# Decay rows in other columns, first weight loads issued earlier, other fillers and new priority tables in a fused attention, gate and MLP kernel

## The chip, the cores and the metric

The kernel runs on one core of one Trainium2 chip. A core has TensorE (PE in the rows; PEld is its weight load), VectorE (DVE), ScalarE (ACT), GpSimd (POOL) and SyncE (SP), which work side by side, each in its own order, and wait for each other by semaphores. DMA engines move data; nearly all transfers here are issued from SP's queue. The metric is the device time of one execution in microseconds; lower is better.

## The reference, cut to what matters

```python
# q, k, v: [4, 8, 576, 64]; s: [4, 8, 576]
scores = q @ k.T / 8                                   # per batch and head
cum = np.cumsum(np.maximum(s, 0), -1)
scores = where(causal, -1e9, scores + np.minimum(-(cum[..., :, None] - cum[..., None, :]), 0))
attn = exp(scores - max(scores)); attn /= sum(attn) + 1e-9
x = (attn @ v) as [4, 576, 512]
gate = sigmoid(sum over k < 5 of conv_w[k] * x shifted by 4 - k tokens)
x = (gate * (x @ w_val)) @ w_out
u = x + (x.T @ U @ V).T                                # U: [576, 32], V: [32, 576]
out = u + relu(u @ w_ch1) @ w_ch2                      # 512 -> 2048 -> 512
```

The weights of all steps behind the attention (conv_w, w_val, w_out, U, V, w_ch1, w_ch2) come as 64-bit numbers, which the kernel turns into pairs of 32-bit ones on the chip ("widening" in what follows). Matrix products are made of three products each: high by high, high by low and low by high part.

## The kernel before, in words

Features lie on the 128 partitions and tokens on the columns. `uT`, a tile of 4 x (4 batches x 576) columns, is where each batch's result is built; columns that no batch uses yet serve as scratch.

**Decay.** The decay bias of a score enters the score product as extra rows: each head's Q and K tile have 64 rows of data and four (two for heads 0 and 1) of decay. For heads 2 to 31 these rows are E and F, made once for all 32 heads from `s` by a cumulative sum (`sp`, `cum`, `ones`) and stored to a DRAM tile `ef`, from where each head loads its own. Before the change `sp` and `cum` lie in batch 1's columns of `uT`, E in batch 2's and F in batch 3's.

**Heads.** A loop over phases n = 0 to 32 emits the scores of head n (`score`, five query tiles, S0 to S4: TensorE product `sc`, DVE maximum `P<-sc`, ACT exp) and, for the head before, its transposes (`trans`, T0 to T4: `pt<-ident,P` on TensorE, then a copy into PTA or PTB). Behind each second head come, for the pair of heads, the product with V (`attn_v`, into `av`, the one PSUM accumulator of its kind), the row sums (`norm_rows`: `rs`, `wrs`), and `norm`: DVE multiplies `av` by the rows into X; POOL splits X into `xh` and `xl`; ACT starts the gate with the first tap into the same accumulator, four DVE taps follow (`av<-X,cw,av`), and ACT's tanh (`uT<-av`) ends it and frees the accumulator. Four pairs are a batch. When a batch's heads are done, its dense work (`values`: x @ w_val and the gate; `outputs`: w_out, U and V) runs between the scores of the next.

**Fillers.** `fill` puts matmuls of zeros (`pt<-causal`) ahead of transposes in the first phases: `fill(bank[key], 2)` for each new tile of transposes and two for each of `norm_rows`, for phases up to 2.

**Side work.** `side_work` is a queue of small steps that widen the weights: conv_w (`craw` to `cw`), then eight chunks of w_val and w_out, U and V, then halves of w_ch1 and w_ch2 (`hraw`). Per 128 x 512 chunk: POOL or ACT scale and limit, four DVE passes (lines 493, 494, 497 and 498 of the kernel before; 504, 505, 508 and 509 of the changed one), three more on POOL. `SIDE` says how many steps a head takes: `[7, 6, 2, 9]` for four ranges of heads. The raw chunks lie in a ring of three, and conv_w beside it, in batch 2's columns of `uT`. The first loads are issued in phases 1 to 3.

**Order.** `Via(kind)` gives each kind of instruction an engine and a priority from the tables PLAN, FIRST (phases up to 8) and LAST (phase 32); a scheduler places the instructions by these priorities. Every instruction that it records has the line of `Via`'s call, 250 before and 255 after, so rows are told apart by their tiles. SP issues loads in its own order, and each engine executes in order.

**MLP.** Behind the last head the MLP runs to the end, from about 350 us on; its first part overlaps with the last heads' work.

Of the kernel before, what the change touches and what calls it, by code (L numbers as in the profile page):

```python
# [20 lines left out]


PLAN = {'pace': ['gpsimd', 0],
 'qk_hi': ['gpsimd', 500],
 'qk_lo': ['gpsimd', -2000],
 'put': ['sync', 2000],
 'wd_rest': ['gpsimd', -500],
 'xh': ['gpsimd', 2000],
 'xl': ['gpsimd', 2000],
 'gh': ['scalar', 0],  # L30
 'gl': ['vector', -6000],
 'uh': ['vector', 500],
 'ul': ['gpsimd', -500],
 'u4': ['vector', 100],
 'wd_a': ['scalar', 0],
 'wd_lim': ['gpsimd', 500],
# [6 lines left out]
 't': ['tensor', 100],
 'pt10': ['scalar', 6000],
 'pt20': ['scalar', -6000],
 'pt30': ['scalar', 100],
 'pt40': ['scalar', -500],
 'pt41': ['vector', 100],
 'av': ['tensor', 2000],
 'rs': ['vector', 100],  # L50
 'wrs': ['gpsimd', 6000],
 't_rb': ['tensor', 500],
 'rb': ['scalar', -2000],
 'x': ['vector', 500],
 'tap0': ['scalar', 2000],
 'tap': ['vector', -2000],
 'tanh': ['scalar', 2000],
 'd': ['tensor', -2000],
 'gv': ['vector', 500],
 'ox': ['scalar', 2000],  # L60
 'tm': ['tensor', 0],
 'nh': ['scalar', 0],
 'nl': ['vector', 100],
 'ah': ['vector', 100],
 'al': ['vector', 100],
 'um': ['vector', 500],
 'c1': ['tensor', -2000],
 'c2': ['tensor', -6000],
 'hh': ['scalar', -100],
 'hl': ['vector', 2000],  # L70
 'acc': ['vector', -100],
 'tc': ['vector', -6000],
 'th': ['scalar', 2000],
 'tl': ['vector', 2000],
 'sc': ['gpsimd', -2000],
 'sh': ['scalar', 100],
 'sl': ['gpsimd', 6000],
 'sn': ['scalar', 2000],
 'sa': ['vector', -6000],
 'tu': ['tensor', 6000],  # L80
 'tv': ['tensor', -500],
 'fetch': ['sync', -6000],
 'te': ['vector', 0],
 'tle': ['gpsimd', 2000],
 'the': ['scalar', -500]}
# [14 lines left out]
PACE = 1  # L100
PLACE = [[0, 2, 1, 4, 3], [0, 1, 4, 2, 3], [4, 0, 1, 2, 3], [2, 3, 0, 1, 4]]
PACED = False
SIDE = [7, 6, 2, 9]
WHOLE = [0, 1, 2, 3, 4, 5, 6, 7, 16, 30]
XB = 1
FIRST = {'pt41': ['scalar', -6000],
 'nl': ['vector', 500],
 'xh': ['gpsimd', 0],
 'c2': ['tensor', 0],
# [4 lines left out]
 'av': ['tensor', 6000],  # L114
 'wd_rest': ['gpsimd', -2000],
 'ah': ['scalar', -500],
 'pt10': ['scalar', 100],
 'al': ['vector', -500],
 'xl': ['gpsimd', 500],
 'pt40': ['scalar', -6000],  # L120
# [3 lines left out]
 'gh': ['scalar', 500],  # L124
 'hl': ['vector', 0],
 'wd_hi': ['gpsimd', -500],
 'u4': ['gpsimd', -500],
 'pt20': ['scalar', 2000],
 'pace': ['gpsimd', 500],
 'tm': ['tensor', 2000],  # L130
# [8 lines left out]
 'tc': ['gpsimd', -2000],  # L139
 'sn': ['vector', -6000],  # L140
 'sh': ['vector', -500],
 'tu': ['tensor', -6000],
 'tv': ['tensor', 0],
 'qk_hi': ['gpsimd', 100],
 'th': ['scalar', -2000],
# [2 lines left out]
 'ox': ['vector', 500],  # L148
 'wd': ['vector', 0],
 'tanh': ['scalar', 6000],  # L150
 'exp': ['scalar', 0],
 'hh': ['scalar', -2000],
 'ul': ['gpsimd', 6000],
 'sl': ['vector', 0],
 'acc': ['vector', 2000],
 'te': ['gpsimd', -2000],
 'tap0': ['scalar', -6000],
 'wd_lo': ['gpsimd', 2000],
 'tl': ['vector', 2000],
# [41 lines left out]
DT = {'exp': 0.71,
 'xh': 0.51,
 'xl': 1.47,
 'tap': 2.23,
 'taps': 0.51,
 'tanh': 1.21,
 'gv': 1.47,
 'nl': 3.07,
 'rows': 9.44,
 'prep': 3.98}  # L210
WARM = 13


@with_exitstack
def fused_kernel(ctx, tc, qT, kT, vP, s, wval, wout, convw, U, V, w1, w2, rows01, out):
# [495 lines left out]
    def norm_rows(pr):  # L711
        force("sc")
        sm = sums[pr % 2]
        rs = at1.tile([P, 5, 2], F32, tag="rs", name="rs", bufs=2)
        Via("rs").tensor_scalar_add(rs, sm, 1e-9)
        Via("rs").reciprocal(rs, rs)
        wide_rs = at1.tile([P, 5, P], F32, tag="wrs", name="wrs")
        rnd("wrs", wide_rs.rearrange("p c (e d) -> p c e d", e=2), rs.unsqueeze(3).to_broadcast([P, 5, 2, 64]))
        ready.add(("rows", pr))
        RB = RBs[pr] = wide_rs.rearrange("p c q -> p (c q)")[:, 0:S]  # L720
        for lo, hi, cs in ((0, SA, (0, 1, 2)), (SA, S, (3, 4))):
            ps = psD.tile([P, 512], F32, tag="d", name="pt")
            fill(ps, 2)
# [660 lines left out]
```

## Time and profile before

| | |
|---|---|
| time, median of 3 runs | 738.66 us (737.77 to 739.78) |
| profiled execution's own time | 739.64 us |
| span of the profile | 737.9 us |
| mean granted TensorE clock | 0.981 of full speed |
| busy: PE, DVE, ACT, POOL | 711.0, 566.9, 323.5, 242.4 us |
| DMA | 92.96 MB, mean 126 GB/s |

The span is from the first to the last instruction; the execution's own time has launch and end around it. Busy time counts instructions of an engine, idle time ahead of one is put down to what it waited for, and PEclk is the share of full clock that TensorE was granted.

### The profile page before, as it was taken

To read this page: it belongs to the slowest core of one execution; us is meant where nothing else is said; L and a number is where in the kernel's file an instruction comes from. 1 tells how busy PE (TensorE), PEld (TensorE's weight loads), DVE (VectorE), ACT (ScalarE), POOL (GpSimd) and SP (SyncE) were. 2 spreads that over 40 slices of the span, in tenths; PEclk is the share of its full clock that TensorE was granted. 3 is DMA by queue.
4 is the path that set the end of the run, shared out by engine and by line. 5 is a ranking of instruction groups with operands and counts; after the bars stand their busy time and mean duration, and the time that the engine had idled before them with its cause. 6 is when DMAs were issued, how large, how long until landed. Compare 5 with 4: busy or idle time off the path is not lost.

```text
span 737.9 us, 12465 instructions
## 1 busy us (share of the span) xinstructions
PE 711.0 (96%) x4395; PEld 600.6 (81%) x4395; DVE 566.9 (77%) x1279; ACT 323.5 (44%) x786; POOL 242.4 (33%) x269
## 2 busy tenths in 40 slices
PE   8987899899899999999999999999999999999997
PEld 4765799679888999799878888888888888888886
DVE  6688797878778765783599888898989899686454
ACT  5676476746667667752242222322222223132220
POOL 2567577645453433378060111011020111001000
PEclk8898999979999999999999999999999999999999
DMA  4675555744566553035201222616327062350063
GB/s 129 193 203 152 148 144 141 184 113 111 145 154 155 148 131 92 33 96 190 87 1 57 89 84 74 240 58 229 113 86 257 29 225 91 106 177 1 15 213 143
DMA packets 43130, 92.96 MB, mean 126 GB/s; under 512 B 6440, under 2 KB 7080, under 8 KB 43068
## 3 DMA queue, kind: packets, MB, share of 16 engines
q1 hardware_dynamic: 43068, 92.17, 41.9%
q8 instruction: 35, 0.57, 0.3%
q14 instruction: 27, 0.22, 0.1%
HBM read 66.40 MB, written 9.50 MB: 103 GB/s over the span
## 4 chain that ended last, share of the span: by engine, by line
PE 80%; DVE 9%; DMA 4%; ACT 4%; POOL 2%; issue 1%; SPq 0%; POOLq 0%; ACTq 0%
PE d L250 36%; PE acc L250 26%; PE av L250 6%; PE pt L250 5%; PE sc L250 5%; DMA uT<-in_w 2%; DVE P L250 1%; DVE av L250 1%; POOL uT L250 1%; DVE sn L250 1%; DMA K<-Q 1%; ACT P L250 1%; PE pt L830 1%; DVE uT L250 1%; DVE uT L493 1%
## 5 line engine op out<-in xcount | busy, mean ns | idle before, releaser
L250 DVE TENSOR_TENSOR uT<-acc,uT 128x512 f32<-128x512 f32 (+1 forms) x160 | 96.0, 629 | 29.2 <-PE acc L250 28.4
L250 PE MATMUL acc<-hl,w2h 128*128 128x512 f32 (+1 forms) x320 | 103.8, 370 | 0.0
L250 PE MATMUL acc<-hh,w2l 128*128 128x512 f32 (+1 forms) x320 | 102.8, 371 | 0.0
L250 PE MATMUL acc<-hh,w2h 128*128 128x512 f32 (+1 forms) x320 | 102.1, 371 | 0.0
L250 PE MATMUL sc<-K,Q 68*128 68x288 f32 (+13 forms) x384 | 92.7, 353 | 1.8 <-ACT PTB L250 1.1
L250 PE MATMUL d<-u,w1h 128*128 128x512 f32 (+1 forms) x320 | 84.1, 350 | 0.0
L250 DVE CUSTOM_DVE_ANT_0 P<-sc,causal 64x64 f32<-64x64 f32 (+4 forms) x160 | 65.0, 421 | 23.5 <-PE sc L250 22.9
L250 PE MATMUL pt<-ident,P 128*128 128x128 f32 x400 | 66.6, 287 | 8.4 <-DVE nm L250 3.4
L250 POOL TENSOR_SCALAR scr<-raw 128x512 f32<-128x512 f32 x28 | 20.0, 715 | 157.0 <-DVE w1l L250 80.6
L250 ACT ACTIVATE P<-P,nm 64x64 f32<-64x64 f32 (+4 forms) x115 | 63.8, 557 | 17.0 <-DVE nm L250 16.7
L250 PEld LDWEIGHTS sc<-K,Q 68*128 68x128 f32 (+2 forms) x384 | 63.2, 198 | 8.8 <-DVE nm L250 1.9
L250 PEld LDWEIGHTS acc<-hh,w2h 128*128 128x128 f32 x320 | 59.1, 188 | 11.7 <-ACT Sh L257 0.4
L250 PEld LDWEIGHTS acc<-hh,w2l 128*128 128x128 f32 x320 | 59.1, 188 | 11.2
L250 PEld LDWEIGHTS acc<-hl,w2h 128*128 128x128 f32 x320 | 59.0, 188 | 11.0 <-DVE hl L250 0.2
L250 PEld LDWEIGHTS pt<-ident,P 128*128 128x128 f32 x400 | 48.7, 146 | 18.9 <-ACT P L629 5.2
L250 PEld LDWEIGHTS d<-u,w1h 128*128 128x128 f32 x320 | 56.0, 188 | 9.2 <-DVE hl L250 0.2
L250 ACT ACTIVATE hh<-sn 128x512 fp32r<-128x512 f32 x47 | 28.8, 630 | 67.8 <-DVE sn L250 50.9
L250 DVE SCALAR_TENSOR_TENSOR av<-X,cw,av 128x576 f32<-128x576 f32 x64 | 52.2, 815 | 4.8 <-ACT av L250 4.4
L250 PE MATMUL d<-u,w1l 128*128 128x512 f32 (+1 forms) x160 | 55.8, 349 | 0.0
L250 ACT ACTIVATE sn<-d 128x512 f32<-128x512 f32 x39 | 23.3, 597 | 72.2 <-PE d L250 69.5
L250 POOL TENSOR_TENSOR Sl<-scr,Sh 128x512 fp32r<-128x512 f32 x14 | 18.5, 1327 | 95.6 <-ACT Sh L257 95.6
L250 ACT ACTIVATE hh<-d 128x512 fp32r<-128x512 f32 (+1 forms) x41 | 20.8, 511 | 62.6 <-PE d L250 34.7
(187 smaller groups left out, 1690.8 us busy)
## 6 DMA issues: line engine op xcount, KB each, us to landing
raw<-in_w SPq DMA_DIRECT2D x28, 512.0 KB
Eh<-te SPq DMA_DIRECT2D x48, 256.0 KB
El<-te SPq DMA_DIRECT2D x48, 256.0 KB
V<-in_vP SPq DMA_DIRECT2D x16, 576.0 KB
K<-hi SPq DMA_DIRECT2D x44, 144.0 KB
Q<-hi SPq DMA_DIRECT2D x44, 144.0 KB
out<-uT SPq DMA_DIRECT2D x16, 256.0 KB
qk<-in_qT SPq DMA_DIRECT2D x22, 144.0 KB
```

The lines of the kernel that those rows point to most:

```text
L250: return f(*args, **kw)
L493: lambda: Via("wd").tensor_scalar(tu, au, 3, None, op0=ALU.logical_shift_left),
L830: Via("tm").transpose(ps[:, m * P:(m + 1) * P], uT[:, m, s0:s0 + P], ident)
```

## The change

- `sp` and `cum` go into a tile `early` in a PTB buffer, `ones` into a PTA buffer; E and F go into the columns of batches 0 and 1. The columns of the ring and of `craw` are so free from the start.
- conv_w and the first two chunks of w_val (`SOON = 2`) are issued in the code ahead of the store of `ef`; the scheduler puts a third chunk there too. Side steps are also taken in phase 0.
- `SIDE` becomes `[9, 8, 2, 9]`.
- `FILL = [4, 3, 1]`: four fillers for a tile of transposes, and only in phases up to 1; the three of `norm_rows` never come, since it runs from phase 2 on. Twenty fillers become twelve.
- `ORDER0`, PLAN, FIRST, LAST and the scheduler's delays DT have other numbers; some kinds change engine.

```diff
-PLAN = {... 'wd_a': ['scalar', 0], 'wd_lim': ['gpsimd', 500], 'tap': ['vector', -2000], ...}
+PLAN = {... 'wd_a': ['scalar', 2000], 'wd_lim': ['gpsimd', 6000], 'tap': ['vector', -500], ...}
...
+SOON = 2
-SIDE = [7, 6, 2, 9]
+SIDE = [9, 8, 2, 9]
...
-ORDER0 = 'S0 T0 T1 T4 S1 S2 T3 T2 S3 S4'
+ORDER0 = 'S0 S1 T0 T4 T1 S2 T2 T3 S3 S4'
...
-DT = {'exp': 0.71, 'xh': 0.51, 'tap': 2.23, 'tanh': 1.21, 'gv': 1.47, 'prep': 3.98, ...}
+DT = {'exp': 0.93, 'xh': 0.43, 'tap': 2.2, 'tanh': 0.99, 'gv': 2.35, 'prep': 1.43, ...}
+FILL = [4, 3, 1]
...
-    sp, cum = (part(1, m, parts=NH) for m in range(2))
-    ones = part(1, 2)
+    early_t = at.tile([P, 5 * (S - SA)], F32, tag="PTB", name="early")
+    sp, cum = (early_t[0:NH, m * S:(m + 1) * S] for m in range(2))
+    ones = at.tile([P, 4 * DA], F32, tag="PTA", name="ones")[:, 0:S]
-    E = [part(2, r, parts=NH) for r in range(KP)]
-    F = [part(3, r, parts=NH) for r in range(KP)]
+    E = [part(0, r, parts=NH) for r in range(KP)]
+    F = [part(1, r, parts=NH) for r in range(KP)]
...
+    ring = [uT[:, m, 2 * S:2 * S + 1024] for m in range(3)]
+    craw = uT[:, 3, 2 * S + 1024:2 * S + 1064]
+    nc.sync.dma_start(craw.bitcast(U32), convw.bitcast(U32))
+    for i in range(SOON):
+        nc.sync.dma_start(ring[i].bitcast(U32), wval.bitcast(U32)[i * P:(i + 1) * P, :])
     for i in range(2):
         nc.sync.dma_start(ef[:, i], EF[i])
...
-        if phase[0] <= 2:
+        if phase[0] <= FILL[2]:
...
-            fill(bank[key], 2)
+            fill(bank[key], FILL[0])
...
-        if n == 1:
-            nc.sync.dma_start(craw.bitcast(U32), words(convw))
-        if 1 <= n <= 3:
+        if max(1, SOON) <= n <= 3 and n > SOON:
             load_wide(n - 1)
...
-            if n > 0:
+            if n > 0 or SOON:
                 steps[0] += SIDE[(n > 8) + (n > 12) + (n > 17)] * cost / total
```

Where the order changes, three places are shown, as they stand in the two programs. The first is SP's queue near the start, behind the loads of Q and K of heads 0 and 1; `V` is the value tile of heads 0 and 1, the loads from `in_qT` and `in_kT` are head 2's. Before:

```order
L418 DMA V<-in_vP 128x1152
L473 DMA ef<-uT 32x4x576 x2
L407 DMA Q_196<-in_qT 64x576
L408 DMA K_197<-in_kT 64x576
L413 DMA Q_196<-uT 4x1x576
L413 DMA K_197<-uT 4x1x576
L925 DMA uT<-in_convw 128x40
L521 DMA uT<-in_wval 128x1024 x2
```

After:

```order
L480 DMA uT<-in_convw 128x40
L482 DMA uT<-in_wval 128x1024 x2
L424 DMA V<-in_vP 128x1152
L530 DMA uT<-in_wval 128x1024
L484 DMA ef<-uT 32x4x576 x2
L413 DMA Q_209<-in_qT 64x576
L414 DMA K_210<-in_kT 64x576
L419 DMA Q_209<-uT 4x1x576
L419 DMA K_210<-uT 4x1x576
L530 DMA uT<-in_wval 128x1024
```

conv_w and two chunks now stand ahead of V, a third ahead of the store of `ef`, and a fourth behind head 2's rows.

The second is DVE within the second pair's taps; `X_94` is that pair's product, `av<-X_94,cw,av` its taps, the `ISA P_..` rows are maxima of a head's query tiles and the `ISA nm` rows their results. Before, from behind the second of four taps on:

```order
L250 ISA P_88,nm<-sc,causal 64x64
L250 ISA nm 64x1
L493 TENSOR_SCALAR uT<-uT 128x512
L250 ISA P_92,nm<-sc,causal,nm 128x288
L250 ISA nm 128x1
L250 SCALAR_TENSOR_TENSOR av<-X_94,cw,av 128x576
L494 SCALAR_TENSOR_TENSOR uT<-uT 128x512
L250 ISA P_89,nm<-sc,causal 128x192
L250 ISA nm 128x1
L250 ISA P_90,nm<-sc,causal 128x320
L250 ISA nm 128x1
L250 SCALAR_TENSOR_TENSOR av<-X_94,cw,av 128x576
```

After, from behind the first tap on:

```order
L255 ISA P_88,nm<-sc,causal 64x64
L255 ISA nm 64x1
L255 SCALAR_TENSOR_TENSOR av<-X_94,cw,av 128x576
L255 ISA P_92,nm<-sc,causal,nm 128x288
L255 ISA nm 128x1
L255 SCALAR_TENSOR_TENSOR av<-X_94,cw,av 128x576
L255 ISA P_89,nm<-sc,causal 128x192
L255 ISA nm 128x1
L504 TENSOR_SCALAR uT<-uT 128x512
L255 ISA P_90,nm<-sc,causal 128x320
L255 ISA nm 128x1
L255 SCALAR_TENSOR_TENSOR av<-X_94,cw,av 128x576
```

Two widening passes stood between the taps; now one does, ahead of the last.

The third is TensorE at the start of the products of `values` for batch 0, where `xh_943` (before) and `xh_962` (after) belong to the fourth pair and the others to the first three. Before:

```order
L250 MATMUL d<-xh_405,wvh 128x288
L250 MATMUL d<-xl_406,wvh 128x288
L250 MATMUL d<-xh_405,wvl 128x288
L250 MATMUL d<-xh_577,wvh 128x288
L250 MATMUL d<-xl_578,wvh 128x288
L250 MATMUL d<-xh_577,wvl 128x288
L250 MATMUL d<-xh_746,wvh 128x288
L250 MATMUL d<-xl_747,wvh 128x288
L250 MATMUL d<-xh_746,wvl 128x288
L250 MATMUL d<-xh_943,wvh 128x288
```

After, from behind the first 24 products of the same kind on:

```order
L255 MATMUL d<-xh_761,wvh 128x288
L255 MATMUL d<-xl_762,wvh 128x288
L255 MATMUL d<-xh_761,wvl 128x288
L255 MATMUL d<-xh_413,wvh 128x288
L255 MATMUL d<-xl_414,wvh 128x288
L255 MATMUL d<-xh_413,wvl 128x288
L255 MATMUL d<-xh_588,wvh 128x288
L255 MATMUL pt<-ident,P_88 128x128
L255 MATMUL pt<-ident,P_89 128x128
L255 MATMUL pt<-ident,P_90 128x128
L255 MATMUL d<-xh_962,wvh 128x288 x3
```

The first product with the fourth pair's `xh` was the tenth; now 31 products of the first three pairs stand ahead of it.

## Rows read from the trace of the kernel before

**Rows 1.** Cores view: span and mean granted clock.
```profile
core 0: 737.9 us, clock 0.981
```

**Rows 2.** Windows by stage: us, busy PE, PEld, DVE, ACT, POOL, PEclk, DMA share, GB/s.
```profile
8.60:13.20 4.60, 3.39 (x18) 2.10 (x17) 4.06 (x18) 3.73 (x11) 0.00 (x0) 0.99 0.46 102
13.20:23.40 10.20, 10.20 (x39) 7.67 (x37) 3.39 (x19) 5.86 (x20) 2.28 (x5) 0.50 0.69 204
23.40:38.00 14.60, 14.60 (x110) 10.65 (x108) 12.04 (x36) 9.94 (x29) 9.68 (x12) 1.00 0.53 162
...
67.70:74.60 6.90, 4.67 (x34) 3.37 (x34) 5.22 (x13) 3.37 (x9) 4.54 (x5) 0.51 0.68 179
...
84.00:145.00 61.00, 59.79 (x502) 53.51 (x500) 49.76 (x139) 43.88 (x123) 43.01 (x50) 1.00 0.58 147
145.00:149.70 4.70, 2.72 (x15) 1.65 (x13) 3.90 (x14) 2.39 (x8) 2.39 (x3) 1.00 0.62 134
149.70:160.00 10.30, 9.48 (x42) 6.91 (x41) 6.40 (x18) 4.17 (x13) 3.11 (x5) 0.50 0.25 69
...
350.00:700.00 350.00, 349.18 (x1678) 289.57 (x1677) 289.73 (x514) 97.91 (x172) 50.12 (x50) 1.00 0.31 106
```

**Rows 3.** Waits of PE, 24 to 84 us: in total, times, longest.
```profile
PE av L250 <- ACT uT L250: 3.7, 3, 2.2
PE pt L250 <- ACT P L629: 2.7, 4, 1.3
PE d L250 <- POOL xh L250: 2.5, 1, 2.5
```

**Rows 4.** Timeline, 9 to 24 us: start, duration, instruction, idle time before it.
```profile
19.73 0.53 PE L250 MATMUL sc<-K,Q 68*128 68x64 f32 x2
...
20.44 0.16 DVE L493 TENSOR_SCALAR uT<-uT 128x20 uint32<-128x20 uint32 x1
...
21.29 0.17 DVE L501 TENSOR_TENSOR cw<-uT 128x20 f32<-128x20 f32 x1
21.33 1.06 PE L250 MATMUL pt<-causal 128*128 128x256 bf16 x4
```

**Rows 5.** Tile causal as PE's operand (fillers): ns min/median/max, first and last start.
```profile
L250 PE MATMUL pt<-causal x20: 269/352/421, 10.6 to 28.5; 128*128 128x256 bf16 x20
```

**Rows 6.** Windows of 2 us near the start, columns as in rows 2.
```profile
8.00:10.00 2.00, 1.66 (x6) 0.76 (x4) 1.93 (x3) 0.62 (x1) 0.00 (x0) 1.00 0.05 21
...
18.00:20.00 2.00, 2.00 (x9) 1.47 (x8) 0.99 (x4) 0.76 (x3) 0.41 (x2) 0.50 0.98 338
```

**Rows 7.** Timeline, 49 to 72 us: widening passes, third product, tanh, attn_v.
```profile
51.32 0.68 DVE L494 SCALAR_TENSOR_TENSOR uT<-uT 128x512 uint32<-128x512 uint32 x1
...
59.13 0.74 DVE L250 TENSOR_TENSOR X<-av,wrs 128x576 f32<-128x576 f32 x1
...
62.77 1.39 DVE L494 SCALAR_TENSOR_TENSOR uT<-uT 128x512 uint32<-128x512 uint32 x1
...
67.51 0.68 DVE L498 SCALAR_TENSOR_TENSOR uT<-uT 128x512 f32<-128x512 uint32 x1
...
70.39 0.65 ACT L250 ACTIVATE uT<-av 128x576 f32<-128x576 f32 x1 [0.84 <-DVE av L250]
...
71.09 1.12 PE L250 MATMUL av<-PTA,V 128*64 128x256 f32 x4 [2.23 <-ACT uT L250]
```

**Rows 8.** Timeline, 77 to 84 us: products of batch 0 and the fourth xh.
```profile
79.03 0.29 PE L250 MATMUL d<-xh,wvh 128*128 128x288 f32 x1
...
80.09 0.29 PE L250 MATMUL d<-xh,wvl 128*128 128x288 f32 x1
...
82.14 0.67 POOL L250 TENSOR_SCALAR xh<-X 128x576 fp32r<-128x576 f32 x1
...
82.86 0.54 PE L250 MATMUL d<-xh,wvh 128*128 128x288 f32 x2 [2.49 <-POOL xh L250]
```

**Rows 9.** Timeline, 140 to 150 us: ACT at a w1 half.
```profile
147.17 0.43 ACT L257 ACTIVATE uT<-uT 128x256 f32<-128x256 f32 x1 [2.16 <-DMA uT<-in_w]
```

More of the change, by code (lines that the diff above doesn't have):

```diff
@@ L23 @@
 PLAN = {'pace': ['gpsimd', 0],
- 'qk_hi': ['gpsimd', 500],
- 'qk_lo': ['gpsimd', -2000],
+ 'qk_hi': ['gpsimd', -6000],
+ 'qk_lo': ['gpsimd', -100],
  'put': ['sync', 2000],
@@ L29 @@
  'xl': ['gpsimd', 2000],
[L30 to L36, printed above, removed]
+ 'gh': ['scalar', -500],
+ 'gl': ['vector', 100],
+ 'uh': ['vector', 2000],
+ 'ul': ['gpsimd', 500],
+ 'u4': ['vector', -100],
+ 'wd_a': ['scalar', 2000],
+ 'wd_lim': ['gpsimd', 6000],
  'wd': ['vector', 0],
@@ L42 @@
  'exp': ['scalar', 100],
[L43 to L50, printed above, removed]
+ 't': ['tensor', 6000],
+ 'pt10': ['scalar', 0],
+ 'pt20': ['scalar', 2000],
+ 'pt30': ['scalar', -6000],
+ 'pt40': ['scalar', 0],
+ 'pt41': ['vector', -500],
+ 'av': ['tensor', 100],
+ 'rs': ['vector', 500],
  'wrs': ['gpsimd', 6000],
  't_rb': ['tensor', 500],
- 'rb': ['scalar', -2000],
+ 'rb': ['scalar', 0],
  'x': ['vector', 500],
  'tap0': ['scalar', 2000],
- 'tap': ['vector', -2000],
+ 'tap': ['vector', -500],
  'tanh': ['scalar', 2000],
@@ L59 @@
  'gv': ['vector', 500],
- 'ox': ['scalar', 2000],
+ 'ox': ['scalar', 6000],
  'tm': ['tensor', 0],
- 'nh': ['scalar', 0],
- 'nl': ['vector', 100],
+ 'nh': ['scalar', 2000],
+ 'nl': ['vector', 0],
  'ah': ['vector', 100],
[L65 to L71, printed above, removed]
+ 'al': ['vector', 6000],
+ 'um': ['vector', 0],
+ 'c1': ['tensor', 2000],
+ 'c2': ['tensor', -500],
+ 'hh': ['scalar', -500],
+ 'hl': ['vector', 100],
+ 'acc': ['vector', -500],
  'tc': ['vector', -6000],
- 'th': ['scalar', 2000],
+ 'th': ['scalar', 0],
  'tl': ['vector', 2000],
- 'sc': ['gpsimd', -2000],
+ 'sc': ['gpsimd', -500],
  'sh': ['scalar', 100],
  'sl': ['gpsimd', 6000],
- 'sn': ['scalar', 2000],
- 'sa': ['vector', -6000],
+ 'sn': ['scalar', -100],
+ 'sa': ['vector', 6000],
  'tu': ['tensor', 6000],
  'tv': ['tensor', -500],
[L82 to L85, printed above, removed]
+ 'fetch': ['sync', 100],
+ 'te': ['vector', 6000],
+ 'tle': ['vector', 0],
+ 'the': ['scalar', 0]}
 R0 = 0.31
@@ L116 @@
  'ah': ['scalar', -500],
- 'pt10': ['scalar', 100],
+ 'pt10': ['scalar', 2000],
  'al': ['vector', -500],
@@ L126 @@
  'wd_hi': ['gpsimd', -500],
- 'u4': ['gpsimd', -500],
+ 'u4': ['gpsimd', -100],
  'pt20': ['scalar', 2000],
@@ L141 @@
  'sh': ['vector', -500],
- 'tu': ['tensor', -6000],
+ 'tu': ['tensor', 6000],
  'tv': ['tensor', 0],
@@ L150 @@
  'tanh': ['scalar', 6000],
- 'exp': ['scalar', 0],
+ 'exp': ['scalar', -2000],
  'hh': ['scalar', -2000],
@@ L155 @@
  'acc': ['vector', 2000],
- 'te': ['gpsimd', -2000],
+ 'te': ['vector', -2000],
  'tap0': ['scalar', -6000],
@@ L160 @@
  'sc': ['vector', -500],
- 'tle': ['gpsimd', 6000],
- 't_rb': ['tensor', 6000]}
-ORDER0 = 'S0 T0 T1 T4 S1 S2 T3 T2 S3 S4'
+ 'tle': ['vector', 6000],
+ 't_rb': ['tensor', 6000],
+ 'uh': ['vector', -6000],
+ 's': ['tensor', 500]}
+ORDER0 = 'S0 S1 T0 T4 T1 S2 T2 T3 S3 S4'
 ORDER = 'T0 S0 T1 T3 T2 S1 S2 S3 T4 S4 A0 A1'
@@ L171 @@
  'c2': ['tensor', -6000],
- 'acc': ['vector', -500],
+ 'acc': ['vector', 6000],
  'sh': ['scalar', 0],
  'c1': ['tensor', -500],
- 'sc': ['vector', 500],
+ 'sc': ['vector', -6000],
  'nh': ['scalar', 100],
@@ L180 @@
  'wd_lo': ['vector', -2000],
- 'tc': ['vector', -2000],
- 'wd_lim': ['vector', -6000],
+ 'tc': ['vector', 100],
+ 'wd_lim': ['vector', 0],
  'tl': ['vector', -6000],
- 'hl': ['vector', 100],
+ 'hl': ['vector', 0],
  'the': ['scalar', 500],
  'pt10': ['vector', 6000],
- 'ul': ['gpsimd', 500],
+ 'ul': ['gpsimd', 6000],
  'sl': ['gpsimd', -100],
@@ L192 @@
  'ah': ['scalar', 0],
- 'hh': ['scalar', -100],
+ 'hh': ['scalar', -2000],
  'sn': ['scalar', 100],
- 'wrs': ['vector', 2000],
+ 'wrs': ['gpsimd', 2000],
  'tle': ['gpsimd', 6000],
@@ L198 @@
  'te': ['gpsimd', -6000],
- 'xh': ['scalar', 6000]}
+ 'xh': ['scalar', 6000],
+ 'qk_hi': ['gpsimd', -6000]}
 NPD = 6
-DT = {'exp': 0.71,
- 'xh': 0.51,
+DT = {'exp': 0.93,
+ 'xh': 0.43,
  'xl': 1.47,
[L204 to L207, printed above, removed]
+ 'tap': 2.2,
+ 'taps': 0.58,
+ 'tanh': 0.99,
+ 'gv': 2.35,
  'nl': 3.07,
  'rows': 9.44,
- 'prep': 3.98}
+ 'prep': 1.43}
 WARM = 13
+FILL = [4, 3, 1]
 @with_exitstack
@@ L378, in fused_kernel @@
         nc.scalar.activation(x[64:66, :], x[64:66, :], AF.Relu)
-    EF = [uT[0:NH, :, b * S:(b + 1) * S] for b in (2, 3)]
+    EF = [uT[0:NH, :, b * S:(b + 1) * S] for b in (0, 1)]
     hd = {}
@@ L515, in fused_kernel @@
     scr = [uT[:, 3, 2 * S + i * 512:2 * S + (i + 1) * 512] for i in range(2)]
-    craw = uT[:, 3, 2 * S + 1024:2 * S + 1064]
-    ring = [uT[:, m, 2 * S:2 * S + 1024] for m in range(3)]
     def rows(w, src, c):
@@ L722, in norm_rows @@
             ps = psD.tile([P, 512], F32, tag="d", name="pt")
-            fill(ps, 2)
+            fill(ps, FILL[1])
             for c in cs:
```

2 lines of the change are left out of this document (1 added, 1 removed).

## The prediction

> **What bounds the kernel now.** I read the span and the clock first [rows 1]: 737.9 us at a mean granted clock of 0.981. The profiled execution's own time is 739.64 us, so 1.74 us lie around the span; the median of the runs shown is 738.66 us, 1.0 below this execution. I make the sum against 739.64 and take 1.0 off at the end.
>
> Next comes the table by stage [rows 2]. From 350 to 700 us TensorE (PE) is busy for 349.18 of 350 us, and from 84 to 145 us for 59.79 of 61. There nothing on another engine can be gained or, within limits, lost. Time can only come from TensorE's own work, from its idle time in the first 84 us and around 145 us, and from the three stretches in which PEclk reads 0.50 or 0.51. That is the lower of its two levels, 1.2 instead of 2.4 GHz. What TensorE did there would have taken half as long at the upper level, so the three cost half of its busy time: 10.20/2 = 5.1 us (13.2 to 23.4), 4.67/2 = 2.3 (67.7 to 74.6) and 9.48/2 = 4.7 (149.7 to 160), together 12.1 us. Each follows a stage in which TensorE idled: it was busy for 3.39 of 4.60 us before the first and for 2.72 of 4.70 before the third [rows 2].
>
> Third, whom TensorE waits for between 24 and 84 us [rows 3]: 3.7 us, in three waits, for the tanh on ACT that ends a pair's gate and so frees the one attn_v accumulator; 2.7 us for exps; 2.5 us, in one wait, for the split xh on POOL (GpSimd). These are the waits that the change can reach.
>
> **The change, part by part.**
>
> *Earlier loads.* The E and F rows move out of the columns that the ring of raw weights uses, so conv_w and three w_val chunks (0.52 MB each, 128 x 1024 words of 4 bytes) are issued ahead of the store of ef and of head 2's Q and K. They then lie in a hole: from 8 to 10 us the DMA engines are busy for 0.05 of the time [rows 6]. Three chunks are 1.57 MB; at the 338 GB/s that the same rows show from 18 to 20 us that is 4.7 us of transfer, begun at about 8 us and so done at about 13. Head 2's first score runs at 19.73 us [rows 4]. I cost the loads at nothing. If that cover were gone, head 2 would start up to 4.7 us late.
>
> *conv_w's passes.* The five small DVE passes that widen conv_w take 0.87 us, from 20.44 to the end of the one at 21.29 [rows 4], where TensorE is the bound. They move to the head of the program: two stand ahead of head 0's first maximum, three among its maxima. There the chain scores, maxima, exps has nothing to hide them. Two of five are 0.35 us, all five 0.87. I take **+0.6**. The first also comes to depend on conv_w's load (rival E).
>
> *Filler matmuls.* Twenty of 128 x 256 become twelve. The twenty lie between 10.6 and 28.5 us, with a median of 352 ns [rows 5]; at half clock four in a row took 1.06 us, 0.265 each [rows 4]. In the order before, four stand ahead of head 0's first transposes, ten more up to those of head 1, and six behind; after, eight stand ahead of head 0's first, where TensorE idles, and four more up to head 1's. So six fewer run in the slow stretch, in which TensorE was busy for all of 10.20 us [rows 2]: 6 x 0.265 = 1.6. The bounds are 0, if TensorE then waits for exps instead, and 8 x 0.265 = 2.1. I take **-1.5**. The last six I cost at nothing, since waits lie beside them; without these waits they would add at most 6 x 0.13 at full clock.
>
> *Widening earlier and faster* (SIDE from 7 to 9 steps a head, and from head 0). DVE is in order, so a 128 x 512 pass between two taps puts off the tanh, and with it the next pair's attn_v. In the third pair the product is at 59.13, the tanh at 70.39, and attn_v starts at 71.09 after 2.23 us of idle time [rows 7]. By the order before, two widening passes stand between the first pair's product and its last tap, two in the second pair, four in the third; after: none, one, three. The second pair loses the pass that took 0.68 (at 51.32); of the third I take the one at 67.51, also 0.68, since the 1.39 of 62.77 stays in another place [rows 7]. Both fit into waits: of the 3.7 us for tanh [rows 3] 2.2 are the third pair's and 1.5 remain for the other two. With 0.7 + 0.7, and 0.2 for the first pair, whose wait is the smallest, I take **-1.6**. The bounds are 0 (the pairs' maxima put off the last tap instead) and all of 3.7.
>
> *Order of the dense work of batch 0.* Before, nine products of `values` stand ahead of the first that needs the fourth xh. They start at 79.03 and 80.09 (first and last: 0.133 apart), then TensorE waits for POOL, whose xh starts at 82.14 and lets it go on at 82.86, after 2.49 us [rows 8]. After, 31 products that need only the first three pairs stand ahead: 31 x 0.133 = 4.1 us, where 82.86 - 79.03 = 3.8 are wanted. So the wait is covered: **-2.4**. The bounds are 0, if POOL's xh comes later by as much, and -2.5. What is behind it runs with TensorE nearly full from 84 us on [rows 2], so the gain is kept.
>
> *The rest.* PTA copies going from ACT to DVE, the limits and raw copies on POOL, the tables for the heads after 84 us, and the changed priorities of the MLP I cost at nothing, because TensorE is full there; if that cover failed, single waits of half a microsecond would show. The three slow stretches I leave where they are, since what precedes each stays: the wait for the first exps, the third pair's maxima, and the load at 145 us.
>
> Sum: 0.6 - 1.5 - 1.6 - 2.4 = -4.9; 739.64 - 4.9 = 734.7, and 1.0 less is **733.7 us**.
>
> **The rivals.** Two times within 0.3% (2.2 us) I count as the same: from 736.4 to 740.9 us.
>
> *B. One slow stretch goes as well.* The third follows a wait of ACT: the ACTIVATE at 147.17 sits 2.16 us idle for the load of a w1 half, with exps behind it [rows 9]. In the new order load and ACTIVATE stand among other work; with five ACT instructions more between them the wait would be gone, and with it the idle time before the clock falls. For the first stretch, four more fillers stand in the idle time before it. Against: the load is still issued one step ahead of its first use, and four fillers at full clock fill little of the 1.2 us idle in the 4.60 [rows 2]. It gives 4.7 to 5.1 us more: 733.7 - 5 = 728.7.
>
> *C. The gains are not there.* TensorE's waits for tanh and xh are replaced by waits for exps, because DVE and POOL get 9 steps of widening a head instead of 7 and the maxima queue behind them. For: the exps already cost 2.7 us [rows 3]. Against: TensorE has the work to cover it in `values`. Only the fillers' 1.5 less 0.6 remain: about 738.
>
> *D. The clock stays low beyond 23.4 us: slower.* Between 13.2 and 23.4 us the fillers fill TensorE's gaps, and the clock rose after a stretch in which it was busy for all of 10.20 us [rows 2]. With six fewer it may show gaps there and stay at 1.2 GHz. From 23.4 to 38 us it is busy for all 14.60 us [rows 2], so each further microsecond at half clock costs half a microsecond. To lose 4.9 + 2.2 it must stay low for 14 us more; two more lengths of 10.2 give +10.2 and 743.9, one length 738.8. Against: the scores and transposes alone queue there, and DVE waits for them. The Trainium skill (TensorE: Matmul & The Clock Gate, HAM oscillation) says that waits which leave TensorE idle in a loop send its clock down again, each time it has recovered. What it would make of the time here is D's 743.9, and by it taking out fillers is a step in the wrong direction. The trace agrees in so far as the falls follow stages with idle time, but it shows the fall at 13.2 with the fillers in place.
>
> *E. conv_w comes late.* DVE's second instruction on it stands ahead of head 0's first maximum. If its load lands behind the Q and K rows of both heads, DVE waits and all of the prologue with it. Landing 3 to 4 us late gives 733.7 + 3.5 = about 737. Against: it is issued ahead of the chunks and is small.
>
> **How the numbers follow.** Forecast A 0.45 (730.5 to 736.4 by its terms' bounds), B 0.20, C 0.18, D 0.10, E 0.07. The likeliest gives 733.7. For 8 in 10 the range must take in B and C and the short form of D: 727 to 740.5, which leaves out some 0.07 below (two stretches gone, or one with the full bounds) and 0.12 above. Faster: A and B, 0.65; same: most of C and E, and the short form of D, 0.20; slower: the long D and the worst of C, 0.15.
>
> **What would show it.** Right: the fillers' busy time between 13 and 24 us falls by about 1.5 us; TensorE's wait for the third pair's tanh falls from 2.23 to about 1.5, and the one for the fourth xh from 2.49 to under 0.3; the three slow stretches are still there and begin within 5 us of where they were, less what was gained ahead; behind 160 us nothing differs by more than 1 us. Wrong: a stretch at half clock more or fewer, a DVE wait for conv_w ahead of the first maximum, waits of TensorE for exps that grow by what those for tanh shrink, or idle time of TensorE in the MLP.

## The result, and the profile after

The changed kernel takes 730.57 us (median of 6 runs, 728.65 to 731.72) against 739.12 us of the kernel before (6 runs, 737.77 to 740.09): ratio 0.9883, interval 0.9862 to 0.9904. That is 8.5 us less, where 4.9 were worked out. The direction and the range held; much of the size came from places where the prediction had put nothing. A ratio, here and below, leaves out runs more than 1.5% above the fastest of their program, and it is not the quotient of the two medians.

The cores view of the changed kernel's profile and two of its windows by stage, with the columns and limits of [rows 2]:

```profile
core 0: 729.3 us, clock 0.988
```

```profile
84.00:145.00 61.00, 55.59 (x449) 48.97 (x448) 48.86 (x136) 39.75 (x114) 37.10 (x44) 1.00 0.58 147
...
350.00:700.00 350.00, 349.21 (x1676) 289.71 (x1675) 291.41 (x515) 96.64 (x169) 48.71 (x49) 1.00 0.32 108
```

The span fell by 8.6 us [rows 1]. The MLP from 350 us on is what it was, 349.21 us busy of 350. The stage from 84 to 145 us is less full than before, 55.59 against 59.79 us [rows 2]. There are again three stretches at half clock, 1.7 to 5.1 us earlier than before, and two of them are shorter. Their own windows:

```profile
11.44:14.85 3.41, 3.41 (x14) 2.29 (x13) 2.32 (x12) 3.16 (x13) 1.27 (x2) 0.50 0.93 334
66.05:69.46 3.41, 2.89 (x26) 2.13 (x28) 0.89 (x4) 1.34 (x3) 2.80 (x4) 0.50 0.70 215
144.56:154.80 10.24, 9.80 (x44) 7.30 (x42) 6.51 (x23) 4.16 (x12) 2.91 (x5) 0.50 0.21 59
```

10.2, 6.8 and 10.2 us at the lower level have become 3.4, 3.4 and 10.2. By half of TensorE's busy time they cost 12.1 us before and (3.41 + 2.89 + 9.80)/2 = 8.1 after. The difference is half of what the span lost, and the prediction had left it at zero.

TensorE's waits from 24 to 84 us in the changed kernel, beside [rows 3]:

```profile
PE av L255 <- ACT uT L255: 4.6, 2, 3.9
PE pt L255 <- ACT P L255: 1.3, 2, 1.1
...
PE d L255 <- POOL xl L255: 0.2, 1, 0.2
```

The wait for the fourth xh (2.5 us) is gone; 0.2 us for its low part is left. The waits for exps halved. Those for tanh, from which I expected 1.6 us, grew from 3.7 to 4.6: the longest, the third pair's, grew from 2.2 to 3.9, and the others fell from 1.5 to 0.7 together. The timeline of the third pair shows how, beside [rows 7]:

```profile
53.59 0.75 DVE L255 TENSOR_TENSOR X<-av,wrs 128x576 f32<-128x576 f32 x1
...
57.31 1.35 POOL L255 TENSOR_SCALAR uT<-uT 128x512 f32<-128x512 f32 x2
...
58.69 0.43 DVE L504 TENSOR_SCALAR uT<-uT 128x512 uint32<-128x512 uint32 x1 [1.55 <-POOL uT L255]
...
59.73 1.41 POOL L255 TENSOR_TENSOR xl<-X,xh 128x576 fp32r<-128x576 f32 x1
...
60.34 1.35 DVE L505 SCALAR_TENSOR_TENSOR uT<-uT 128x512 uint32<-128x512 uint32 x1
...
65.87 0.65 ACT L255 ACTIVATE uT<-av 128x576 f32<-128x576 f32 x1 [1.43 <-DVE av L255]
...
66.57 2.19 PE L255 MATMUL av<-PTA,V 128*64 128x256 f32 x20 [3.89 <-ACT uT L255]
```

The product (X) stands 5.5 us earlier than in [rows 7], and the tanh only 4.5. DVE sits idle for 1.55 us at 58.69, in its order, for POOL's scaled chunk of 57.31, and the tap behind it is late; three passes stand between taps, as the order said, and the second of them takes 1.35 us. TensorE's wait for this tanh grew from 2.23 to 3.89 us.

The products of `values` for batch 0, beside [rows 8]:

```profile
76.64 0.67 POOL L255 TENSOR_SCALAR xh<-X 128x576 fp32r<-128x576 f32 x1
...
78.24 0.29 PE L255 MATMUL d<-xh,wvh 128*128 128x288 f32 x1
...
78.62 0.64 PE L255 MATMUL d<-xh,wvh 128*128 128x288 f32 x3
```

The 31st product begins at 78.24, and the first with the fourth pair's xh at 78.62 has no wait, for POOL began that xh at 76.64.

The second place where time came from lies behind the ninth pair's product, at about 180 us. TensorE's waits from 150 to 230 us, before and then after:

```profile
PE pt L250 <- DVE nm L250: 1.2, 2, 0.9
PE sc L250 <- ACT PTB L250: 1.1, 1, 1.1
PE pt L250 <- ACT P L250: 0.7, 2, 0.4
PE pt L830 <- DVE nm L250: 0.5, 1, 0.5
PE av L250 <- ACT uT L250: 0.4, 1, 0.4
PE d L250 <- ACT PTB L250: 0.2, 1, 0.2
```

```profile
PE av L255 <- ACT uT L255: 0.5, 1, 0.5
PE d L255 <- DVE gvl L255: 0.2, 1, 0.2
PE sc L255 <- DMA qk<-in_kT: 0.2, 1, 0.2
PE pt L255 <- DVE nm L255: 0.2, 1, 0.2
```

Together 4.1 us before, of which 0.8 lie ahead of that product, and 1.1 after, all behind it. What moved is seen at one half of the MLP's weights. Before, on ACT and then on TensorE:

```profile
191.39 0.43 ACT L257 ACTIVATE uT<-uT 128x256 f32<-128x256 f32 x1 [3.74 <-DMA uT<-in_w]
191.73 0.47 ACT L250 ACTIVATE PTB<-pt 128x384 f32<-128x384 f32 x1
```

```profile
192.26 0.54 PE L250 MATMUL sc<-K,Q 68*128 68x288 f32 x2 [1.07 <-ACT PTB L250]
```

After, on ACT:

```profile
185.28 0.44 ACT L255 ACTIVATE uT<-uT 128x256 f32<-128x256 f32 x1 [2.75 <-DMA uT<-in_w]
185.62 0.39 ACT L255 ACTIVATE gvh<-d 128x288 fp32r<-128x288 f32 x1
```

In both kernels ACT waits some 3 us for the load of a half. Before, the copy into PTB is the next instruction on ACT, and TensorE waits 1.07 us for it; after, another instruction stands there, and TensorE has no wait. The tables, which I had costed at nothing because TensorE was full, are the likeliest cause; e4 and e7 below bear on it.

### The profile page after: what moved, and what is told of

The parts are those of the page before. It is cut to its first block, busy times and chain, and to the rows that moved or that the text cites. A ratio compares the mean times of both kernels' runs of the same rounds, so it can differ in the third digit from the quotient of the medians.

```text
span 729.3 us, 12465 instructions
## 1 busy us (share of the span) xinstructions
PE 706.5 (97%) x4387; PEld 597.8 (82%) x4387; DVE 563.2 (77%) x1282; ACT 319.6 (44%) x780; POOL 246.3 (34%) x272
## 4 chain that ended last, share of the span: by engine, by line
PE 80%; DVE 8%; DMA 5%; POOL 3%; ACT 2%; issue 1%; SPq 0%; POOLq 0%; ACTq 0%; DVEq 0%
PE d L255 37%; PE acc L255 26%; PE av L255 6%; PE sc L255 5%; PE pt L255 5%; DMA uT<-in_w 2%; DVE P L255 1%; DMA qk<-in_kT 1%; DVE av L255 1%; DVE sn L255 1%; DMA K<-Q 1%; POOL uT L255 1%; DVE uT L504 1%; PE pt L839 1%; POOL Q L255 1%
## 5 line engine op out<-in xcount | busy, mean ns | idle before, releaser
L255 PE MATMUL acc<-hl,w2h 128*128 128x512 f32 (+1 forms) x320 | 106.2, 371 | 0.0
L255 ACT ACTIVATE P<-P,nm 128x576 f32<-128x576 f32 (+4 forms) x160 | 88.9, 557 | 34.3 <-DVE nm L255 33.6
L255 PEld LDWEIGHTS sc<-K,Q 68*128 68x128 f32 (+2 forms) x384 | 61.4, 194 | 11.8 <-DVE nm L255 4.6
L255 PE MATMUL pt<-ident,P 128*128 128x128 f32 x400 | 64.4, 279 | 3.8 <-ACT P L255 1.9
```

Source lines behind the costliest of these rows:

```text
L255: return f(*args, **kw)
```

## The experiments

The runs came in three groups, each on one chip with runs of the kernel before between them; its medians there were 738.49 (31 runs, 730.71 to 742.95), 738.05 (29 runs, 731.37 to 743.78) and 737.16 us (17 runs, 729.86 to 742.59). So single executions of one program lie 12 to 13 us apart on one chip, far more than in the first six, and their granted clocks go from 0.973 to 0.995: the lower the clock, the longer the run. Ratios are to the kernel before of the same group.

**Both kernels again.** The same programs, with no edit.

> The changed kernel once more, unaltered, on the chip of the runs that stand beside it. If the slow stretches are set by the program, they are at 11.4 (3.4 us), 66.1 (3.4) and 144.6 (10.2) again, and the time is 729 to 732. If they fall by chance, places and lengths differ, and the time less half of TensorE's busy time in them is the number that repeats: 721.2 us of span, within 1 us.

> The kernel before once more, unaltered, one look. If its slow stretches belong to the program, they are at 13.1 (10.2 us), 67.8 (6.8) and 149.7 (10.2) again. If their lengths are drawn anew in each execution, some of the three differ by 3.4 us or more, and behind the ninth pair's product (184.6 us of 737.9) the rest is 553.3 us again, within 1 us.

The changed kernel: 728.69 us (6 runs, 725.38 to 733.01), ratio 0.9888 (0.9836 to 0.9939), profiled span 727.9. The kernel before: one run, 735.11 us, span 733.3. Their stretches at half clock (for the kernel before also the stage of its first one), and in each the product of the ninth pair; first the changed kernel again:

```profile
11.39:14.80 3.41, 3.41 (x15) 2.35 (x14) 2.36 (x12) 3.16 (x13) 1.26 (x2) 0.50 0.95 322
62.59:72.83 10.24, 6.25 (x39) 4.71 (x41) 7.26 (x20) 4.14 (x12) 7.68 (x9) 0.50 0.55 147
127.44:130.85 3.41, 3.41 (x20) 2.47 (x19) 2.53 (x11) 3.26 (x12) 1.53 (x3) 0.50 0.54 164
```

```profile
177.43 0.76 DVE L255 TENSOR_TENSOR X<-av,wrs 128x576 f32<-128x576 f32 x1 [0.29 <-PE av L255]
```

The kernel before again:

```profile
13.20:23.40 10.20, 10.20 (x80) 7.84 (x78) 5.65 (x27) 8.07 (x28) 2.39 (x5) 1.00 0.74 210
65.47:72.30 6.83, 5.66 (x45) 4.04 (x46) 3.69 (x10) 1.52 (x3) 2.96 (x4) 0.50 0.78 196
143.97:154.21 10.24, 9.69 (x42) 7.02 (x41) 6.51 (x18) 4.14 (x13) 3.22 (x6) 0.50 0.26 70
304.40:307.81 3.41, 3.41 (x27) 2.92 (x26) 1.57 (x4) 1.46 (x4) 0.87 (x1) 0.50 0.00 0
```

```profile
179.04 0.76 DVE L250 TENSOR_TENSOR X<-av,wrs 128x576 f32<-128x576 f32 x1 [0.71 <-ACT wrs L250]
```

And that product in the first two profiles:

```profile
184.61 0.76 DVE L250 TENSOR_TENSOR X<-av,wrs 128x576 f32<-128x576 f32 x1 [0.71 <-ACT wrs L250]
```

```profile
178.69 0.76 DVE L255 TENSOR_TENSOR X<-av,wrs 128x576 f32<-128x576 f32 x1 [0.29 <-PE av L255]
```

Which stretches come, and how long they are, differs between executions of one program. The kernel before has none near the start this time, where 10.2 us had cost 5.1, and one more at 304 us; the changed one has 10.2 in place of 3.4 us at 63 and 3.4 in place of 10.2 near 130. What repeats better is the rest: behind the ninth product the kernel before takes 737.9 - 184.6 = 553.3 and 733.3 - 179.0 - 1.7 (the stretch at 304 us) = 552.6 us, the changed one 550.6 and 550.5. So 2.0 to 2.8 us are gained behind it by the order alone. Ahead of it, less half of the busy time in the stretches, the kernel before takes 172.5 and 171.4, the changed one 170.6 and 170.9: 0.5 to 1.9 us. Together that is 2.5 to 4.7 us of order.

The granted clock of every run, which the groups give too, settles this better than four profiles. At like clock, 0.986 to 0.991, 17 runs of the kernel before take 734.1 us on average and 9 of the changed one 729.9: 4.3 us of order. Over all runs that count in ratios, 66 of the kernel before take 736.9 us at a mean clock of 0.985, and 12 of the changed one, the first six among them, take 729.7 at 0.989. So of these 7.3 us some 3 go with the clock, which is higher in the changed kernel.

**The parts, one at a time.** Four kernels undo one part of the change, two do one part alone.

```diff
e1  -FILL = [4, 3, 1]        +FILL = [2, 2, 2]
e2  -SIDE = [9, 8, 2, 9]     +SIDE = [7, 6, 2, 9]
e3  -SOON = 2                +SOON = 0
e4  -PLAN, FIRST, LAST, ORDER0, DT of the changed kernel   +those of before
e7  the kernel before, with PLAN, FIRST, LAST, ORDER0, DT of the changed kernel
e8  the kernel before:  -fill(bank[key], 2)  +fill(bank[key], 4);  -if phase[0] <= 2:  +if phase[0] <= 1:
```

> The changed kernel with the fillers of before (two for each tile of transposes and of the row sums, in phases 0 to 2: twenty in place of twelve). Theory F: the denser fillers ahead of the first transposes are what shortened the first slow stretch from 10.2 to 3.4 us; then it returns to 6.8 or 10.2 us, and the time rises by 1.7 to 3.4 and by the fillers' own 1 to 1.5 us, to 733 to 735.5. Rival T: loads, order and tables shortened it; then it stays at 3.4 us, the eight fillers cost 0.13 us each at most, and the time is 730.6 to 731.6.

> The changed kernel with the old pace of widening, SIDE = [7, 6, 2, 9]. My term: fewer steps put widening passes back between the taps, TensorE's waits for tanh before 84 us rise above 4.6 us in all, and the time is 731.5 to 733.5. Rival: the faster pace is what lengthened the third pair's wait from 2.23 to 3.89 us, since DVE queues behind POOL there; then that wait falls to 2.3 or less, and the time is 728.5 to 730.5, unless a wait for unfinished weights in the dense work of batch 0 takes its place.

> The changed kernel with SOON = 0: the chunks of w_val are issued in phases 1 to 3, as before, and side steps begin in phase 1; conv_w stays early, fillers, pace and tables are the changed kernel's. Theory L: the early chunks and the side steps that they allow carry a good part of the gain, by work on DVE and POOL that lies in the first 24 us instead of between taps; then X of the second and third pair come 2 us or more later and the time is 732.5 to 736. Rival: they are only moved, and the gain is that of the clock; then the first slow stretch stays at 3.4 us and the time is within 1 us of 730.6.

> The changed kernel with the tables of before (PLAN, FIRST, LAST, ORDER0 and the delays DT); columns, early loads, pace and fillers stay changed. Theory T: the tables set TensorE's order and so the first slow stretch and the covered wait for the fourth xh; then the stretch is 6.8 us or longer, the wait is back at 2 us or more, and the time is 735 to 739. Rival: the loads, pace and fillers do it; then the time is 730 to 732.5.

> The kernel before with the changed tables alone (PLAN, FIRST, LAST, ORDER0 and DT); columns, loads, pace and fillers stay those of before. Theory T: the tables carry the gain in TensorE's order; then the wait for the fourth xh falls under 0.5 us and the span less half of the slow stretches' busy time falls from 725.8 by 2.4 or more. Rival: tables and structure are worth something only together, or the structure alone is; then that number is within 1.5 us of 725.8.

> The kernel before with four fillers for each tile of transposes, in phases 0 and 1 only, and with those of the row sums in phase 1 alone, if any. Theory F: denser fillers ahead of the first transposes shorten the slow stretch at 13 us from 10.2 to 3.4 us, and the time falls by 3 to 5 us. Rival: with the old order the stretch stays at 6.8 to 10.2 us, and only the fillers' own time is saved, 1.5 us or less.

| kernel | median us (range) | ratio to before (interval) | mean clock |
|---|---|---|---|
| e1, old fillers | 738.36 (734.20 to 741.69) | 0.9990 (0.9952 to 1.0029) | 0.985 |
| e2, old pace | 736.08 (731.97 to 736.77) | 0.9973 (0.9935 to 1.0011) | 0.984 |
| e3, late loads | 734.47 (733.37 to 739.27) | 0.9984 (0.9946 to 1.0022) | 0.982 |
| e4, old tables | 737.57 (733.24 to 741.06) | 0.9971 (0.9930 to 1.0012) | 0.984 |
| e7, tables alone | 732.76 (730.14 to 739.33) | 0.9950 (0.9910 to 0.9991) | 0.988 |
| e8, fillers alone | 736.85 (734.55 to 743.74) | 1.0005 (0.9969 to 1.0041) | 0.985 |

Any one part undone leaves nothing that these runs can tell from the kernel before, and of the parts alone only the tables gain, some 0.5%. The parts don't add up. Some of that is clock: with a part undone the mean clock is 0.982 to 0.985, that of the kernel before, where the changed kernel has 0.989, a step worth some 3 us above. Most of my theories missed, and the traces show other waits in each, where the scheduler placed other instructions. In e1 the stretch near the start stayed at 3.4 us (against theory F), but a wait of 3.6 us appeared from 150 to 230 us:

```profile
PE pt L255 <- ACT PTA L262: 3.6, 1, 3.6
```

In e2 the third pair's wait for tanh stayed at 3.9 us, neither up (my term) nor down (the rival), and exps became late from 90 to 150 us:

```profile
PE pt L255 <- ACT P L255: 4.0, 2, 3.7
```

In e4, from 24 to 90 us, the wait for the fourth xh is 0.8 us, and one of 2.6 us for a head's decay rows is new. From 150 to 230 us its waits sum to 3.3 us. In e8 the first stretch is 3.4 us long, as theory F has it, and the time is no shorter.

In e3 exps and copies into PTA came late between 90 and 150 us (waits of 3.1 and 2.7 us in all). In e7 the waits from 150 to 230 us sum to 1.4 us, near the changed kernel's 1.1 and 1.6, which with e4's 3.3 points to the tables, though e1 has the tables too and a new wait there. e7's theory held in its profile: there is no wait for the fourth xh, and the span less half of TensorE's busy time in the stretches is 721.3 us, as in the changed kernel (721.2 and 721.4; 725.8 and 723.9 in the kernel before). Its ten runs show a smaller gain, and one profile does not settle that.

**No fillers.**

```diff
-FILL = [4, 3, 1]
+FILL = [0, 0, 1]
```

> The changed kernel with no fillers at all. My rival D and the rule of the clock gate: with gaps where the fillers stood the clock stays low longer near the start, 6.8 us or more of half speed before 30 us, and the time is 2 to 6 us above the changed kernel's 728.7 to 730.6. Other theory: the order of scores and transposes decides; then the first slow stretch is 3.4 us or less and the time is within 2 us, on either side.

745.38 us (4 runs, 742.84 to 746.19), ratio 1.0145 (1.0091 to 1.0199): slower than before by 1.4%, and by 2.6% (1.0145/0.9888) than the changed kernel. TensorE's wait for the first exps, from 8 to 24 us, and the two longest of six stretches at half clock:

```profile
PE pt L255 <- ACT P L255: 2.8, 1, 2.8
```

```profile
13.95:24.19 10.24, 10.14 (x33) 8.00 (x34) 4.07 (x14) 5.48 (x18) 4.86 (x5) 0.50 0.40 120
65.15:82.22 17.07, 12.55 (x65) 9.02 (x67) 13.45 (x35) 7.62 (x22) 14.49 (x15) 0.50 0.37 90
```

Where the fillers stood TensorE waits 2.8 us, then follow 10.2 us at half clock, and 17.1 us more at 65. With fillers, in twelve or twenty, the kernels had 0, 3.4 or 10.2 us near the start. Its four runs had clocks of 0.968 to 0.972. Half of TensorE's busy time in its six stretches is 18.0 us, against 8.1 and 6.5 in the changed kernel, and the rest of the span is 725.0 us, against 721.2 and 721.4: most of the loss is clock. Rival D is so a real mechanism; twelve fillers were enough to keep it away, and none are not. The Trainium skill (TensorE: Matmul & The Clock Gate, HAM oscillation) has the idle waits of a loop send the clock down again and again; this trace agrees in so far as 10.2 us at half clock follow the wait of 2.8.

**Fillers meant for the third pair's wait.**

```diff
+        if prt == 0 and n == 5:
+            ps = psD.tile([P, 512], F32, tag="d", name="wait")
+            for _ in range(28):
+                Via("av").matmul(ps[:, 0:256], warm[:, 0:P], warm[:, 0:256], start=True, stop=True)
```

> The changed kernel with 28 fillers of 128 x 256 straight ahead of the third pair's attn_v, where TensorE waits 3.6 to 3.9 us for the tanh; 28 at 0.107 to 0.13 us are 3.0 to 3.6 us, so they fit into the wait. Theory: the idle time is what the clock falls on; with it filled, no stretch at half clock begins between 60 and 68 us, and the time falls by 1.4 to 3.1 us, half of TensorE's busy time in the stretches there (2.9 and 6.3). Rival: the fall has its cause further ahead, in the waits between 57 and 62 us; then it comes all the same, the fillers run at half clock and beyond the wait, and the time rises by up to 3 us.

732.92 us (12 runs, 730.71 to 738.97), ratio 0.9990 (0.9952 to 1.0024): the gain is lost. But the edit did not reach the wait. It puts the fillers ahead of the third pair's own attn_v, and the wait for that pair's tanh lies one pair on, ahead of the fourth pair's. The fillers, and then the fourth pair's attn_v with its wait:

```profile
51.69 4.76 PE L255 MATMUL wait<-causal 128*128 128x256 bf16 x28
...
73.21 2.19 PE L255 MATMUL av<-PTA,V 128*64 128x256 f32 x20 [1.37 <-ACT uT L255]
```

One stretch at half clock lies at 44.6 us (10.2 us), and the next begins 12 us behind the fillers:

```profile
68.49:78.73 10.24, 7.81 (x53) 5.76 (x53) 6.89 (x21) 4.54 (x12) 8.24 (x10) 0.50 0.63 166
```

So neither theory is tested: what happens when the wait for tanh is filled stays open. The run says only that 28 fillers at this earlier place, 4.76 us of TensorE's time, bring no gain.

**ACT's wait for the halves.** In the changed kernel the instruction on ACT is still there, and in both its profiles TensorE waits 1.7 to 1.8 us for what is queued behind it:

```profile
141.74 0.43 ACT L255 ACTIVATE uT<-uT 128x256 f32<-128x256 f32 x1 [2.13 <-DMA uT<-in_w]
```

Two edits were to take it away; e6 puts empty steps behind the load, e11 moves the pass to POOL.

```diff
e6   -        return [load] + steps + (
     +        return [load, lambda: None, lambda: None] + steps + (
e11  - 'wd_a': ['scalar', 2000],
     + 'wd_a': ['gpsimd', 2000],
```

> The changed kernel with two empty side steps behind the load of each w1 or w2 half, so that ACT's first pass on it stands further behind the load. Theory: ACT's wait of 2.13 us for the load at 141.74 goes, TensorE's wait of 1.81 us behind it too, and the slow stretch at 144.6 (4.9 us of cost) with them, so that the time falls by 2 to 6 us. Rival: other waits of the same size stand there, the stretch stays, and the time is within 1 us of the changed kernel's beside it.

> The changed kernel with the first pass of widening (wd_a) on POOL instead of ACT for heads 9 to 31, so that ACT has no wait for the w1 and w2 halves. Theory: ACT's four waits for them, 7.6 us between 100 and 230 us, go; TensorE's wait of 1.8 us for nh behind the one at 141.74 goes, with the slow stretch that follows it in two of three profiles; the time falls by 1.5 to 5 us. Rival: POOL stands in its own queue and the wait moves to it, with xh and hi behind it; then the stretch stays and the time is the same or up to 3 us more.

e6: 730.36 us (12 runs, 726.43 to 734.58), ratio 0.9891 (0.9856 to 0.9926). Its edit did not reach the wait, since the scheduler set the pass as close behind the load as before (ACT's wait at 144.74 is 2.02 us); so it tells nothing of the theory.

e11: 727.13 us (6 runs, 723.66 to 730.27), ratio 0.9890 (0.9842 to 0.9939). ACT no longer waits for halves, POOL does, from 100 to 230 us:

```profile
POOL uT L255 <- DMA uT<-in_w: 6.1, 4, 2.3
```

TensorE's wait for nh is gone, and in this profile no stretch at half clock lies between 76 and 700 us; but one of 13.7 us came at 45, so that the execution profiled took 730.27 us. The median is the lowest of all, but its interval covers the changed kernel's: not shown to be better.

These two kernels show something else. e6 changes only the steps of the w1 and w2 halves, e11 only heads from 9 on, so near 45 us both are the changed kernel. Yet in e6 TensorE waits there for a head's decay rows (2.25 us in e11), and a stretch at half clock follows:

```profile
43.78 0.41 PE L255 MATMUL sc<-K,Q 68*128 68x64 f32 x2 [2.31 <-DMA K<-ef]
```

```profile
44.68:54.92 10.24, 9.97 (x45) 6.57 (x45) 7.47 (x22) 5.71 (x17) 2.76 (x4) 0.50 0.61 130
```

In the changed kernel's two profiles the same product waits 0.4 and 1.0 us, for exps, and no stretch follows. In e11 the load of these rows was issued at 40.79 us and waited for until 45.34; in the first profile of the changed kernel it was issued at 40.36 and had landed by 43.30. All four profiles with this wait (e4, e6, e11 and e12, 1.6 to 2.6 us) have a stretch of 10.2 or 13.7 us that begins at 42.9 to 45.4 us. So a load that lands later in one execution than in another can be what brings a stretch. This is seen four times, and no edit tested it.

## Why the prediction was right, and where it was wrong

**The sum.** Ahead of the ninth product, where all four terms lie, 0.5 to 1.9 us of the 4.9 came. That the gain of order at like clock, 4.3 us, is near 4.9 all the same is luck: part of it came from a stage that was left at nothing. 730.57 lies at the edge of forecast A, whose terms' own bounds give 730.7 to 739.5; 736.4 is only where "same" begins.

**The stretches at half clock.** "The three slow stretches I leave where they are" is the step that failed. I read them in one profile as parts of the program. In the first profile of the changed kernel their places did hold, within some 5 us, but their lengths did not: the profile of the kernel before on which the sum rests had 27.3 us of them, its second profile 20.5, the changed kernel 17.1 twice. By the clocks of all runs some 3 us between the two kernels go with fewer or shorter ones in the changed kernel. Which part of the change raises its clock is not shown, except that it takes fillers.

**Behind 84 us.** "I cost at nothing, because TensorE is full there" failed too, both ways. From 90 to 150 us TensorE's waits grew from 2.8 to 5.5 us (2.9 and 5.3 in the second profiles), so that what was gained ahead was not all kept. Then 2.0 to 2.8 us came behind the ninth product, as waits of TensorE from 150 to 230 us fell from 4.1 to 1.1 us (4.0 and 1.6 in the second profiles). My own sentence named what failure would show, single waits of half a microsecond, but I had not searched the stage for them. The MLP was right, at nothing.

**Widening (-1.6).** Not there. The first two pairs' waits for tanh did fall, by 0.8 us (0.7 in the second profiles), but the third pair's grew, from 2.2 to 3.9 (3.1 and 3.6). The order told rightly how many passes stand between the taps; it doesn't tell that DVE would stand behind POOL for one of them. The sums are 3.7 and 4.6 in the kernel before, 4.6 and 4.4 in the changed one, so what is shown is no gain, not a loss.

**Values (-2.4).** Right in its mechanism: 31 products cover the wait. The size is 0.9 to 2.5 us, since the kernel before waits only 0.9 there in its second profile.

**Fillers (-1.5).** Their busy time from 13.2 to 23.4 us fell from 2.96 to 0.69, more than the 1.5 named: six fewer at 0.296 are 1.8 of it, and the four that are left ran partly at full clock. The price was one at half clock, and so rested on the stretch that I had left alone: six at full clock are 0.8. Their own time is the lesser part of what they do: without them the kernel is 2.6% slower.

**conv_w (+0.6) and the loads (0).** Right. The first maximum came at 10.27 in place of 10.05, and the last of head 0, with three more passes ahead of it, 0.6 us later; before and after:

```profile
12.02 0.52 DVE L250 CUSTOM_DVE_ANT_0 P<-sc,causal,nm 128x288 f32<-128x288 f32 x1
```

```profile
12.63 0.52 DVE L255 CUSTOM_DVE_ANT_0 P<-sc,causal,nm 128x288 f32<-128x288 f32 x1
```

The loads began in the hole, as said, and kept the DMA engines busy to about 14 us; head 2's first score came at 18.02 in place of 19.73. A window of 2 us:

```profile
10.00:12.00 2.00, 1.46 (x8) 1.15 (x9) 1.97 (x12) 1.90 (x7) 0.36 (x1) 0.86 1.02 419
```

No wait of DVE for conv_w (rival E) is there. Rival B, a stretch less, comes nearest to what happened, but not by its mechanism, since ACT's wait for the half is still there. C is refuted by the time and by the waits for exps, which halved, and D did not come with twelve fillers.

## What to carry to other kernels

Before a sum rests on half-clock stretches of one profile, take a second profile of the same program: they can move and cost 5 us more or less in it. Compare runs at like granted clock, which tells order from clock without a profile. Price an edit on what repeats, here the times between two landmarks with the clock taken out. And where a scheduler sets the order, parts of a change can't be priced one by one: with any one of four parts undone, no gain could be told any more.

## What the runs showed of the hardware

The kernel before had 10.2 us at half clock in its first 24 us in one execution and none in another, and single times of it lie up to 13 us apart on one chip, with granted clocks of 0.973 to 0.995. The DMA engines moved 419 GB/s from 10 to 12 us, where I had taken 338 as their rate [rows 6]. And the second widening pass, with two SBUF inputs, took 1.35 us at 60.34 beside POOL's subtraction of 59.73, as it took 1.39 at 62.77 before, and 0.68 us at 51.32 with nothing on POOL [rows 7]. The Trainium skill (SBUF — State Buffer, Who interferes with whom) says that such a DVE instruction contends with a GpSimd one that reads SBUF, and the trace agrees there.
